# First attention blocks with one wide exponential after the transposition, row sums from a column of ones, batched scalings, signs partly on GpSimd, and another order

## The chip, the cores and the metric

The program runs on one core of one Trainium2 chip. The metric is the device time of one execution in microseconds (us); the time of a kernel is the median of its runs, and smaller is better. TensorE is called PE here, VectorE DVE, ScalarE ACT, GpSimd Pool, and SyncE, which only issues transfers, SP.

## The reference

A windowed attention over 4 batches, 8 heads, 576 positions and 64 channels feeds two feed-forward layers, each with a 512 x 2048 and a 2048 x 512 matrix. All inputs are float32.

```python
scores = (q @ k.T) / sqrt(64)
# heads 0-3: the last 32 positions; heads 4-7: every 4th of the last 128
scores = where(mask, scores, -1e9)
attn = exp(scores - max(scores)); attn = attn / (sum(attn) + 1e-9)
x = concat_heads(attn @ v)                 # 2304 tokens x 512
h = x @ w_in1;  y = (relu(h) ** 2) @ w_out1
h = y @ w_in2;  out = (h * sigmoid(h)) @ w_out2
```

## The kernel before

**Arithmetic.** Inputs of the feed-forward matrices arrive as pairs of 32-bit words and are turned into float32 on the chip; then each float32 matrix is split into a high and a low part of type fp32r, and each product is three matmuls (high x high, high x low, low x high). `weights` (L375 on) does this for one piece of 128 x 512: `top` (L394/L396, ACT or Pool) scales the upper word, L409 (DVE) shifts it left by 3, L411 (DVE) puts the sign bit in, `low` (L402, ACT) scales the lower word, L414 adds the two (DVE or Pool), L360/L364 copy the high part (ACT or Pool), L367 subtracts to get the low part (DVE or Pool). There are 64 pieces, 32 for each layer.

**Attention.** It is cut into 32 blocks: 8 halves of a batch (`h`, 288 positions each) by 4 pairs of heads (`pair`). A block has 3 units of 96 queries (plain heads) or 4 units of 72 queries (dilated heads), and two heads (`par`). Before the change, `attention` does for each block: scores (L563, PE) of all units of both heads; for each head and unit a masked minimum of the negated scores (L585, DVE), then an exponential with that minimum as bias, which also gives the row sum (L590, ACT); for each head one addition (L594), one reciprocal (L596) and for each unit a scaling (L604 ACT, L606 DVE or Pool); the transposition of each unit (L613, PE); a copy of the transposed probabilities out of PSUM (L360 ACT or L362 DVE); and one group of products with the values for both heads (L635, PE), whose result is split into high and low parts of `x`.

**Feed-forward.** Layer 0 has six tiles of tokens, three of 256 (`mlp`: lines L711 to L713 and L759 to L761) and three of 512, layer 1 has four of 512 and one of 256 (`mlp2`: lines L859 and L913 to L915). The first three tiles run while the weights are still being converted, so they run interleaved, each a fixed lag behind the one before. Tile 0 needs half 0 of the attention, tile 1 half 1, tile 2 half 2. From tile 3 on, converted weights are read back from memory.

**Order.** Every operation is an `Op` with a cost for each engine that can do it. `Planner.order` plays the program through with these costs when the kernel is built, takes at each step what can start first (the `key`, multiplied by `KEY_W`, decides near ties), chooses the engine, and so fixes the order on every engine. `lock` marks DVE operations that the planner doesn't let overlap with Pool. A load with a `gate` isn't issued before a given step of the feed-forward part. Up to `FILL_END`, when PE would sit idle in the plan, `fill` puts in matmuls on a tile of zeros (`warm`, L961) whose result nobody reads. `HINTS` moves single operations to an engine or shifts their key. Buffers come from pools: `raw` has 4, `ax` banks of PSUM 3.

Of the kernel before, what the change touches and what calls it, by code (L numbers as in the profile page):

```python
# [10 lines left out]
F32 = mybir.dt.float32  # L11
# [8 lines left out]
BLK_BUFS, BLK_COLS = 2, 1216  # L20
# [16 lines left out]
HOLDS = {"w0": "u4", "wa": "u4", "ws": "u4", "wb": "u4", "wc": "u2", "h": "u4", "xr": "u4", "xo": "u2", "cw": "u2", "raw": "u4", "ap": "u4", "x": "u4", "x2": "u4", "g4": "u4", "st": "u4",  # L37
# [24 lines left out]
def block_cols(half, pair):  # L62

    units = attn_units(half, pair)
    nk = max(u[2] + u[3] for u in units)
    return HALF, nk, len(units) * P
# [29 lines left out]
class Op:  # L96
    def __init__(self, engines, fn, deps, key, allocs, uses):
        self.engines, self.fn, self.key = engines, fn, key
        self.deps = [d for d in deps if d is not None]
        self.allocs, self.uses = allocs, uses  # L100
        tags = [g for b in allocs for g in b.tags]
        self.wants = [(g, tags.count(g)) for g in dict.fromkeys(tags)]
        self.start = self.end = self.eng = self.gate = None
        self.pace, self.full, self.lock = False, True, False
        for b in allocs:
            b.alloc_op = self


class Planner:
# [25 lines left out]
    def order(self):  # L135
# [90 lines left out]
        out, left_n = [], len(self.ops)  # L226
# [3 lines left out]
        while left_n:  # L230
            left_n -= 1
            best = None
            for e, r in ready.items():
                pick = None
                for o, t in r.items():
                    t = at(o, e, t)
                    if t is not None and all(t + o.engines[e] <= at(o, f, ready[f][o]) + d + 1e-9
                                             for f, d in o.engines.items() if f != e):
                        c = (t + KEY_W * o.key, o.seq)
# [11 lines left out]
            o.end = run(t, o.engines[e], o.full) if e == "PE" and t < FILL_END else t + o.engines[e]  # L251
# [58 lines left out]
class Kern:  # L310
    def __init__(self, ctx, tc, qkv, w1, w2, out):
# [10 lines left out]
        for h in range(NH):  # L322
            for pair in range(NPAIR):
                self.off[h, pair] = o
                cq, ck, cv = block_cols(h % 2, pair)
# [44 lines left out]
    def weights(self, m, c, key, dkey, js=(0, 1)):  # L370
# [3 lines left out]
        for j in js:  # L374
# [16 lines left out]
            def top(e, cv=cv, pair=pair):  # L391
# [3 lines left out]
                else:  # L395
                    nc.gpsimd.tensor_scalar(out=cv.tile, in0=x, scalar1=2.0 ** -112, scalar2=1.0,  # L396
                                            op0=ALU.mult, op1=ALU.mult)

            def low(e, pair=pair):
# [3 lines left out]
                else:  # L403
                    nc.gpsimd.tensor_scalar(out=x.bitcast(I32), in0=x, scalar1=2.0 ** -29, scalar2=1.0,
                                            op0=ALU.mult, op1=ALU.mult)

            a = self.op({"ACT": c_act(n) + 0.05, "Pool": c_pool1(n)}, top, [load], k, [cv], [raw], "v" + at)
            z = self.op({"ACT": c_act(n) + 0.05, "Pool": c_pool1(n)}, low, [load], k, [], [raw], "z" + at)
            b = self.op({"DVE": c_dve2(n)}, lambda e, vi=vi: nc.vector.tensor_scalar(  # L409
                out=vi(), in0=vi(), scalar1=3, scalar2=None, op0=ALU.logical_shift_left), [a], k, [], [cv], lock=True)  # L410
            s = self.op({"DVE": c_dve(n)}, lambda e, vi=vi, pair=pair: nc.vector.scalar_tensor_tensor(  # L411
                out=vi(), in0=pair(I32)[:, :, 1], scalar=-2147483648, in1=vi(),
                op0=ALU.bitwise_and, op1=ALU.bitwise_or), [b], k, [], [cv, raw], lock=True)
# [8 lines left out]
            h = self.op({"ACT": c_act(n), "Pool": c_pool1(n)}, lambda e, hv=hv, cs=cs: self.copy(e, hv(), cs()),  # L422
                        [w], k, [both], [cv], "h" + at)
# [95 lines left out]
    def load_blk(self, h, pair, key):  # L519
        nc = self.nc  # L520
        cq, ck, cv = block_cols(h % 2, pair)
# [9 lines left out]
        else:  # L531
# [8 lines left out]
            self.blk[h, pair] = parts[0], [(b, cq, o), (b, cq + ck, o)], parts[1]  # L540

    def attention(self, h, pair, key, step):
# [10 lines left out]
        pp = self.spot("ap", 1024)  # L553
        sp = self.buf("ast", 4, 24, rows=PL_Q)
# [16 lines left out]
        else:  # L571
            s = self.op({"PE": 0.1 + 0.26 * nu if h == 0 else 0.92}, scores, deps, key, sbanks + [pp, sp], use)
            s.full = h == 0
            ss = [s, s]
        for par in range(2):
# [6 lines left out]
            for i, (q0, n, k0, nk, m0) in enumerate(units):  # L582
# [6 lines left out]
                            [s], k + 0.1, [], [sbank, p, st])  # L589
                es.append(self.op({"ACT": c_act(nk) + 0.185}, lambda e, i=i, n=n, c=c, p=p, st=st: nc.scalar.activation(  # L590
                    out=p.tile[:n, c], in_=p.tile[:n, c], func=AF.Exp, scale=-1.0, bias=st.tile[:n, i:i + 1],
                    accum_out=st.tile[:n, 4 + i:5 + i]), [t], k + 0.2, [], [p, st]))
            d = lambda st=st: st.tile[:nq, 8:8 + nu]
# [4 lines left out]
            for i, (q0, n, k0, nk, m0) in enumerate(units):  # L598
                c = slice(i * P, i * P + nk)

                def norm(e, i=i, n=n, c=c, p=p, st=st):
                    x, f = p.tile[:n, c], st.tile[:n, 8 + i:9 + i]
                    if e == "ACT":
                        nc.scalar.activation(out=x, in_=x, func=AF.Copy, scale=f)  # L604
                    else:
                        self.eng[e].tensor_scalar(out=x, in0=x, scalar1=f, scalar2=1.0, op0=ALU.mult, op1=ALU.mult)  # L606

                ns.append(self.op({"Pool": 0.243 + 0.84e-3 * nk, "DVE": c_dve2(nk), "ACT": c_act(nk)}, norm,
                                  [r], k + 0.4, [], [p, st], f"n{at}.{i}", True))
# [27 lines left out]

        k = key + 2 * step
        o = self.op({"PE": 0.75}, pv, pts[0][1] + pts[1][1] + [dv], k,
                    [xb], [bv, pts[0][0], pts[1][0]])  # L640
        self.attended = [o]
# [4 lines left out]
        for t, lo, hi in parts:  # L646
# [33 lines left out]
            a.tagname = f'x{h}.{pair}'  # L680

# [12 lines left out]
    def mlp(self, m, tiles):  # L694
# [3 lines left out]
        for c, ti in sorted(((c, ti) for c in range(NF) for ti in range(len(tiles))), key=lambda x: tiles[x[1]][1](x[0])):  # L698
# [32 lines left out]
            def prod(e, r=r, bank=bank, n=n):  # L731
                if e == "Pool":
                    nc.gpsimd.tensor_tensor(out=r.tile, in0=r.tile, in1=r.tile, op=ALU.mult)
# [7 lines left out]
            b = self.op({"DVE": c_dve(n), "Pool": c_pool2(n)}, prod, [a], k + 0.2, [],  # L741
# [89 lines left out]
    def mlp2(self, m, t, k0, fetched):  # L831
# [7 lines left out]
        for f in range(NF // 2):  # L839
# [47 lines left out]
            for i, (hp, deps, own) in enumerate(parts):  # L887
# [6 lines left out]
                if m == 0:  # L894
                    b = self.op({"DVE": c_dve(n)}, lambda e, r=r, src=src: nc.vector.scalar_tensor_tensor(  # L895
                        out=r.tile, in0=src(), scalar=0.0, in1=src(), op0=ALU.max, op1=ALU.mult),
                        deps, k, [r], [own], f"p{at}.{i}", n == 512)
                else:
# [3 lines left out]
                        out=r.tile, in0=src(), in1=r.tile, op=ALU.mult), [a], k, [], [r, own], f"p{at}.{i}", n == 512)  # L902
# [25 lines left out]
    def constants(self, e):  # L928
        nc = self.nc
        self.ident = self.sb.tile([PL_Q, PL_Q], F32, name="ident")  # L930
        self.mask = self.sb.tile([PL_Q, P], F32, name="mask")
        make_identity(nc, self.ident)
        nc.gpsimd.memset(self.mask, 0.0)
# [6 lines left out]
    def run(self):  # L940
# [54 lines left out]
        for t in range(FIRST, len(TILES[0])):  # L995
# [5 lines left out]
            else:  # L1001
                for c in range(NF):
                    self.weights(1, c, k + 2 * c + 3, k + 2 * c - 1, (1,))
# [11 lines left out]
W_KEY = 4.0  # L1015
A_LEAD = 38.0
B_LEAD = 6.0
A1 = -5.0
A2 = 6.0
A2S = 4.0  # L1020
A3S = 3.0
B_LAG = 14.0
# [3 lines left out]
X_LEAD = 14  # L1026
X1_LEAD = 14
S1_FROM = 27.44
S1_STEP = 3.5
W1_BACK = 40  # L1030
# [4 lines left out]
A0S = 3.0  # L1035
W_STEP = 3.5
W0D = -46.0
B1 = -41.5
A1S = 5.5
W2_FROM = 60.0  # L1040
W2_STEP = 6.0
ENG = {"v": ("Pool", "ACT"), "z": ("ACT",), "w": ("DVE", "Pool"), 
       "h": ("ACT", "Pool"), "S": ("DVE", "Pool"), "l": ("Pool", "DVE"), "n": ("Pool", "ACT", "DVE"), "t": ("ACT", "DVE"), "x": ("DVE", "ACT"), "gh": ("ACT",), "gl": ("DVE", "Pool"), "p": ("DVE",)}
MOST = {"w0": 16, "wa": 3, "ws": 6, "wb": 2, "wc": 3, "h": 1, "xr": 2, "xo": 1, "cw": 2, "raw": 4, "ap": 3, "x": 8, "x2": 14, "g4": 4, "st": 2, "g2": 4, "cv": 3, "r": 2, "yo": 2, "stg": 3}
# [5 lines left out]
    "A5.0": ("", -8.0),  # L1050
    "B3.3": ("", -1.0),
    "R0.4.0": ("", -4.0),
    "gl0.0.10": ("Pool", 0),
    "gl0.5.3.1": ("Pool", 0),
    "h0.14.1": ("", -1.0),
    "n7.3.0.1": ("", 2.0),
    "n7.3.1.3": ("ACT", 0),
    "p0.3.3.1": ("", -1.0),
    "t0.0.1.0": ("", -8.0),
    "v0.15.1": ("ACT", 0),  # L1060
    "xh0.4.b21": ("", 16.0),
    "xh1.3.t2": ("", -2.0),
# [71 lines left out]
```

## Time and profile before

| | us |
|---|---|
| median of 3 runs | 906.86 |
| lowest, highest | 906.71, 909.58 |
| profiled execution, whole | 909.49 |
| profiled execution, span | 907.7 |
| PE busy in the span | 888.2 |
| DVE, ACT, Pool busy | 662.7, 455.0, 78.9 |

The span is what the profiler recorded from the first to the last instruction; 1.8 us of the profiled execution's time lie around it. A busy PE also counts the matmuls on zeros.

### The profile page before, as it was taken

How to read it: one execution, taken by the hardware profiler on the slowest of the kernel's cores; microseconds unless marked ns; L12 is line 12 of the kernel's file. 1: busy time of each engine (PE TensorE's matmuls, PEld its weight loads, DVE VectorE, ACT ScalarE, POOL GpSimd, SP SyncE). 2: the span in 40 equal slices, each digit the busy share in tenths (PEclk: the TensorE clock that was granted, in tenths of full speed). 3: DMA queues.
4: the chain of work that ended last, by engine and by line, in shares of the span. 5: the costliest groups of instructions: out<-in, count | busy, mean ns of one | idle time of the engine just before them, and what ended most of it. 6: DMA issues, size and time to landing. Idle time of an engine off the chain costs nothing.

```text
span 907.7 us, 18193 instructions
## 1 busy us (share of the span) xinstructions
PE 888.2 (98%) x6589; PEld 806.3 (89%) x6589; DVE 662.7 (73%) x1749; ACT 455.0 (50%) x1260; POOL 78.9 (9%) x97
## 2 busy tenths in 40 slices
PE   8999999999999999999999999999999999999998
PEld 6888988999878988899999899999999899999998
DVE  6999999997787798787989986475448445545422
ACT  6979887867675366343454553233225222323222
POOL 1442122110110100010010100000000000000000
PEclk9999999999999999999999999999999999999999
DMA  8487677667989989878889974557565656645060
GB/s 303 157 251 260 206 255 251 238 216 259 335 283 337 344 288 321 310 253 312 306 323 351 368 264 163 200 183 249 170 221 193 201 174 242 244 136 175 26 210 25
DMA packets 75738, 217.92 MB, mean 240 GB/s; under 512 B 8576, under 2 KB 20096, under 8 KB 75648
## 3 DMA queue, kind: packets, MB, share of 16 engines
q1 hardware_dynamic: 75648, 216.76, 68.6%
q8 instruction: 52, 0.85, 0.4%
q14 instruction: 38, 0.31, 0.1%
HBM read 170.59 MB, written 46.14 MB: 239 GB/s over the span
## 4 chain that ended last, share of the span: by engine, by line
PE 74%; DVE 14%; ACT 6%; DMA 4%; issue 2%; SPq 0%; POOL 0%; ACTq 0%; DVEq 0%; POOLq 0%
PE s L859 32%; PE y L913 12%; PE y L914 12%; PE y L915 12%; ACT ap L590 2%; DMA raw<-w 2%; DVE st L367 1%; ACT ap L604 1%; PE ax L961 1%; DVE st L466 1%; DVE g L367 1%; DVE ap L585 1%; DVE ap L606 1%; DVE r L735 1%; DMA x<-xo 1%
## 5 line engine op out<-in xcount | busy, mean ns | idle before, releaser
L875 DVE TENSOR_TENSOR h<-s,h 128x512 f32<-128x512 f32 x224 | 139.5, 623 | 135.2 <-PE s L859 121.7
L913 PE MATMUL y<-g,w 128*128 128x512 f32 (+1 forms) x512 | 194.5, 380 | 0.0
L914 PE MATMUL y<-g,w 128*128 128x512 f32 (+1 forms) x512 | 193.2, 377 | 0.0
L915 PE MATMUL y<-g,w 128*128 128x512 f32 (+1 forms) x512 | 192.8, 377 | 0.0
L859 PE MATMUL s<-x,ws 128*128 128x256 f32 x1344 | 172.4, 283 | 0.7 <-DVE ap L362 0.6
L859 PEld LDWEIGHTS s<-x,ws 128*128 128x128 f32 x1344 | 166.0, 192 | 1.4 <-DVE ap L362 0.7
L360 ACT CAST g<-r 128x512 fp32r<-128x512 f32 (+1 forms) x176 | 94.2, 542 | 58.5 <-DVE r L895 29.0
L915 PEld LDWEIGHTS y<-g,w 128*128 128x128 f32 x512 | 96.4, 188 | 18.4
L913 PEld LDWEIGHTS y<-g,w 128*128 128x128 f32 x512 | 96.5, 188 | 16.1
L914 PEld LDWEIGHTS y<-g,w 128*128 128x128 f32 x512 | 96.5, 189 | 15.3
L367 DVE TENSOR_TENSOR g<-r,g 128x512 fp32r<-128x512 f32 (+1 forms) x170 | 99.5, 605 | 13.8 <-ACT g L360 10.2
L859 PE MATMUL s<-x,wa 128*128 128x256 f32 x768 | 105.0, 285 | 2.0 <-issue 2.0
L859 PEld LDWEIGHTS s<-x,wa 128*128 128x128 f32 x768 | 100.8, 192 | 6.7 <-issue 2.4
L899 ACT ACTIVATE r<-h 128x512 f32<-128x512 f32 x64 | 37.1, 625 | 133.4 <-DVE h L875 133.4
L590 ACT ACTIVATE ap<-ap,ast 96x128 f32<-96x128 f32 (+3 forms) x224 | 82.6, 372 | 17.7 <-DVE ast L585 17.6
L711 PE MATMUL s<-x,w 128*128 128x256 f32 x192 | 56.7, 295 | 3.0 <-DVE ast L585 1.5
L873 ACT COPY h<-s 128x256 f32<-128x256 f32 x56 | 20.7, 370 | 74.5 <-PE s L859 73.1
L901 DVE TENSOR_TENSOR r<-h,r 128x512 f32<-128x512 f32 x64 | 41.5, 689 | 22.6 <-ACT r L899 22.6
L713 PE MATMUL s<-x,w 128*128 128x256 f32 x192 | 54.4, 284 | 0.7 <-DVE w L367 0.7
L712 PE MATMUL s<-x,w 128*128 128x256 f32 x192 | 54.1, 282 | 0.0
L859 PE MATMUL s<-x,wc 128*128 128x256 f32 x336 | 49.3, 282 | 0.0
L402 ACT ACTIVATE raw<-raw 128x512 int32<-128x512 uint32 x64 | 42.6, 678 | 4.6 <-DMA raw<-w 4.6
(110 smaller groups left out, 1452.9 us busy)
## 6 DMA issues: line engine op xcount, KB each, us to landing
raw<-w SPq DMA_DIRECT2D x64, 512.0 KB, 7.2
ws<-w2x SPq DMA_DIRECT2D x64, 512.0 KB, 4.7
ws<-w1x SPq DMA_DIRECT2D x48, 512.0 KB, 6.6
wa<-w2s SPq DMA_DIRECT2D x40, 512.0 KB, 4.2
wa<-w1s SPq DMA_DIRECT2D x24, 512.0 KB, 6.2
w1s<-w SPq DMA_DIRECT2D x16, 512.0 KB, 4.2
w1x<-st SPq DMA_DIRECT2D x16, 512.0 KB, 3.7
w2s<-st SPq DMA_DIRECT2D x16, 512.0 KB, 4.8
```

The source lines that it names most:

```text
L360: self.nc.scalar.copy(out=out, in_=in_)
L367: self.eng[eng].tensor_tensor(out=out, in0=a, in1=b, op=ALU.subtract)
L402: nc.scalar.activation(out=x.bitcast(I32), in_=x, func=AF.Copy, scale=2.0 ** -29)
L590: es.append(self.op({"ACT": c_act(nk) + 0.185}, lambda e, i=i, n=n, c=c, p=p, st=st: nc.scalar.activation(out=p.tile[:n, c], in_=p.tile[:n ...
L711: nc.tensor.matmul(o, wh.tile[:, s], xh, start=(kk == 0), stop=False)
L712: nc.tensor.matmul(o, wh.tile[:, s], xl, start=False, stop=False)
L713: nc.tensor.matmul(o, wl.tile[:, s], xh, start=False, stop=(kk == KC - 1))
L859: nc.tensor.matmul(bank.tile[:, o:o + 256], wp, xp, start=i == 0, stop=last, skip_group_check=True)
L875: add = lambda o, a, b: nc.vector.tensor_tensor(out=o, in0=a, in1=b, op=ALU.add)
L913: nc.tensor.matmul(o, wh.tile[:, s], gh.tile, start=c == 0, stop=False)
L914: nc.tensor.matmul(o, wh.tile[:, s], gl.tile, start=False, stop=False)
L915: nc.tensor.matmul(o, wl.tile[:, s], gh.tile, start=False, stop=(c == NF - 1))
```

## The change

- In the first 8 blocks (halves 0 and 1, `EARLY`), the exponentials move behind the transposition (`late_exp`). PE transposes the shifted scores and adds, in the same PSUM bank, a matmul that subtracts each row's minimum (a column of `ast`, broadcast, times `minus`, the negated identity). One exponential then covers all units of a head that have the same number of keys, reads PSUM and writes SBUF; it has no bias pointer and no row sum. The copy out of PSUM goes away.
- The values of these blocks carry a column of ones for each unit and head (`ones`, a memset), so that the product with the values gives 64 columns and the row sum; it is done for each head apart and comes out with the queries on the partitions. The addition and the reciprocal are as before; one multiplication for each head scales the result of all units into `xn`, and PE transposes it back (`turn`).
- In the other 24 blocks, scalings of units with the same number of keys are one operation; on DVE one multiplication by a broadcast column.
- In `weights`, the operation L409 can go to Pool: it then clears the upper word except for its sign, and the shift is done by DVE together with the sign. `top`, `low` and the high copy can go to DVE too. The square of layer 0's first tiles can go to ACT, no longer to Pool.
- The planner takes 0.17 us off a PE operation that follows one of the same `kind` (scores, and the last PE step of a block) and favours it by 0.31 us in its choice; fillers also wait for an `ax` bank. Leads, lags and the 16 hints are replaced; there are now about a hundred hints.

```diff
-BLK_BUFS, BLK_COLS = 2, 1216
+BLK_BUFS, BLK_COLS = 2, 1224
+EARLY = 8
...
-                t = max(free["PE"], vacant(tag, "PE"))
+                t = max(free["PE"], vacant(tag, "PE"), vacant("ax", "PE"))
...
-                        c = (t + KEY_W * o.key, o.seq)
+                        c = (t + KEY_W * o.key - (STAY if o.kind and o.kind == kind else 0), o.seq)
...
-            o.end = run(t, o.engines[e], o.full) if e == "PE" and t < FILL_END else t + o.engines[e]
+            d = o.engines[e] - (SWITCH if o.kind and o.kind == kind else 0)
+            o.end = run(t, d, o.full) if e == "PE" and t < FILL_END else t + d
...
+            def shift(e, vi=vi, pair=pair):
+                x = pair(U32)[:, :, 1].bitcast(F32)
+                if e == "DVE":
+                    nc.vector.tensor_scalar(out=vi(), in0=vi(), scalar1=3, scalar2=None, op0=ALU.logical_shift_left)
+                else:
+                    nc.gpsimd.tensor_scalar(out=x, in0=x, scalar1=0.0, scalar2=1.0, op0=ALU.mult, op1=ALU.mult)
+            b = self.op({"DVE": c_dve2(n), "Pool": c_pool1(n)}, shift, [a], k, [], [cv, raw], "b" + at, True)
+            def sign(e, vi=vi, pair=pair, b=b):
+                x = pair(I32)[:, :, 1]
+                if b.eng == "DVE":
+                    nc.vector.scalar_tensor_tensor(out=vi(), in0=x, scalar=-2147483648, in1=vi(),
+                                                   op0=ALU.bitwise_and, op1=ALU.bitwise_or)
+                else:
+                    nc.vector.scalar_tensor_tensor(out=vi(), in0=vi(), scalar=3, in1=x,
+                                                   op0=ALU.logical_shift_left, op1=ALU.bitwise_or)
...
+            if early(h, pair):
+                pts.append(self.late_exp(units, p, st, tbank, es, k, at, par, bv, ov, dv, xn))
+                continue
...
+                    if e == "DVE" and j > i + 1:
+                        nc.vector.tensor_tensor(out=x, in0=x, in1=f.unsqueeze(2).to_broadcast([n, j - i, nk]), op=ALU.mult)
+                        return
...
+        def turn(e):
+            for i, (q0, n, k0, nk, m0) in enumerate(units):
+                nc.tensor.transpose(xb.tile[:, q0:q0 + n], xn.tile[:n, i * P:i * P + P], self.ident[:n, :n])
...
+        if early(h, pair):
+            o = self.op({"PE": 0.25}, turn, pts + [self.ident_op], k, [xb], [xn])
+        else:
+            o = self.op({"PE": 0.75}, pv, pts[0][1] + pts[1][1] + [dv], k,
+                        [xb], [bv, pts[0][0], pts[1][0]])
+        o.kind = 1
...
+    def late_exp(self, units, p, st, tbank, deps, k, at, par, bv, ov, dv, xn):
+        nu, nq = len(units), units[0][1]
+        full = max(((i, u[3]) for i, u in enumerate(units)), key=lambda x: (x[1], -x[0]))
+        def transp(e):
+            for i, (q0, n, k0, nk, m0) in sorted(enumerate(units), key=lambda u: -u[1][3]):
+                o = tbank.tile[:nk, q0:q0 + n]
+                nc.tensor.matmul(o, p.tile[:n, i * P:i * P + nk], self.ident[:n, :n], is_transpose=True,
+                                 start=(i, nk) == full, stop=False, skip_group_check=True)
+                nc.tensor.matmul(o, st.tile[:n, i:i + 1].to_broadcast([n, nk]), self.minus[:n, :n],
+                                 start=False, stop=True, skip_group_check=True)
...
+            es.append(self.op({"ACT": c_actp(c.stop - c.start)}, lambda e, c=c, nk=units[i][3]: nc.scalar.activation(
+                out=p.tile[:nk, c], in_=tbank.tile[:nk, c], func=AF.Exp, scale=-1.0), [t], k + 0.3, [], [tbank, p]))
...
+                nc.tensor.matmul(vb.tile[:n, 65 * i:65 * i + 65], p.tile[:nk, q0:q0 + n], bv.tile[:nk, v0:v0 + 65],
+                                 start=True, stop=True)
...
+            if e == "DVE":
+                nc.vector.tensor_tensor(out=x, in0=v()[:, :, :64], in1=d().unsqueeze(2).to_broadcast([nq, nu, 64]), op=ALU.mult)
+                return
+            for u in range(nu):
+                nc.scalar.activation(out=x[:, u], in_=v()[:, u, :64], func=AF.Copy, scale=d()[:, u:u + 1])
...
-X_LEAD = 14
+STAY = 0.31
+SWITCH = 0.17
+X_LEAD = 39.0
...
-B1 = -41.5
+B1 = -31.16
...
-W2_FROM = 60.0
+W2_FROM = 49.2
```

## Rows read from the trace of the kernel before

**Rows 1.** The page: busy time, share of the span and instructions of each engine.
```profile
PE 888.2 (98%) x6589; PEld 806.3 (89%) x6589; DVE 662.7 (73%) x1749; ACT 455.0 (50%) x1260; POOL 78.9 (9%) x97
```

**Rows 2.** Windows: stretch, length; busy of PE, PEld, DVE, ACT, POOL; PEclk, DMA share, GB/s.
```profile
0.00:80.00 80.00, 74.65 (x757) 63.41 (x758) 69.63 (x333) 65.52 (x260) 25.77 (x34) 1.00 0.71 236
80.00:300.00 220.00, 211.86 (x1909) 195.54 (x1908) 196.34 (x683) 160.53 (x531) 32.08 (x40) 1.00 0.77 267
520.00:860.00 340.00, 340.00 (x2138) 308.89 (x2138) 193.13 (x310) 109.84 (x203) 4.06 (x5) 1.00 0.56 192
...
20.00:30.00 10.00, 9.46 (x106) 7.38 (x106) 9.41 (x55) 9.27 (x40) 3.35 (x4) 1.00 0.05 20
```

**Rows 3.** Groups of PE instructions by line, 0 to 80 us.
```profile
L961 PE MATMUL ax<-warm 128*128 128x256 bf16 x237 | 30.9, 281 | 1.1 <-DVE warm L952 1.1
```

**Rows 4.** Timeline of PE: start, length, line and operation.
```profile
4.02 2.61 PE L563 MATMUL y<-w 128*96 128x96 f32 x24
8.78 1.23 PE L563 MATMUL y<-w 128*72 128x72 f32 x16 [2.14 <-DMA w<-qkv]
...
30.06 0.72 PE L635 MATMUL ax<-ap,blk 128*64 128x96 f32 x12
30.70 0.39 PE L711 MATMUL s<-x,w 128*128 128x256 f32 x1
30.92 0.28 PE L712 MATMUL s<-x,w 128*128 128x256 f32 x1
...
35.99 0.90 PE L563 MATMUL ax<-blk 64*96 64x128 f32 x12
36.82 0.39 PE L759 MATMUL y<-g,w 128*128 128x256 f32 x1
...
40.98 0.66 PE L613 MATMUL ax<-ident,ap 96*128 96x96 f32 x6
41.48 0.82 PE L961 MATMUL ax<-warm 128*128 128x256 bf16 x6
```

**Rows 5.** Timeline of ACT: two exponentials of plain heads, one of dilated heads.
```profile
6.02 0.39 ACT L590 ACTIVATE ap<-ap,ast 96x128 f32<-96x128 f32 x1
...
6.41 0.39 ACT L590 ACTIVATE ap<-ap,ast 96x128 f32<-96x128 f32 x1
...
21.37 0.35 ACT L590 ACTIVATE ap<-ap,ast 72x72 f32<-72x72 f32 x1
```

**Rows 6.** Groups by line and shape, ACT, 0 to 100 us: copies out of PSUM.
```profile
L360 ACT COPY ap<-ax 72x288 f32<-72x288 f32 x8 | 3.1, 393 | 0.0
L360 ACT COPY ap<-ax 128x192 f32<-128x192 f32 x7 | 2.3, 327 | 0.0
```

**Rows 7.** Groups by line and shape, DVE: 0 to 300 us, 0 to 80, 0 to 100.
```profile
L409 DVE TENSOR_SCALAR cv<-cv 128x512 int32<-128x512 int32 x38 | 15.8, 433 | 0.5 <-ACT cv L394 0.3
...
L606 DVE TENSOR_SCALAR ap<-ap,ast 96x128 f32<-96x128 f32 x17 | 5.0, 324 | 0.0
...
L367 DVE TENSOR_TENSOR x<-ax,x 128x192 fp32r<-128x192 f32 x4 | 1.7, 432 | 0.4 <-ACT x L360 0.4
```

**Rows 8.** Timelines of DVE (two additions of one shape), of Pool; Pool's group, 0 to 100.
```profile
10.73 0.64 DVE L594 TENSOR_SCALAR ast<-ast 96x3 f32<-96x3 f32 x1
...
13.23 0.15 DVE L594 TENSOR_SCALAR ast<-ast 96x3 f32<-96x3 f32 x1
...
10.70 0.65 POOL L396 TENSOR_SCALAR cv<-raw 128x512 f32<-128x512 f32 x1 [8.60 <-DMA raw<-w]
...
L396 POOL TENSOR_SCALAR cv<-raw 128x512 f32<-128x512 f32 x14 | 13.0, 929 | 28.4 <-DMA raw<-w 20.0 <-PE y L761 4.4 <-DVE cv L409 4.0
```

**Rows 9.** Timeline of PE around 512 us, and windows there.
```profile
512.33 1.57 PE L859 MATMUL s<-x,wa 128*128 128x256 f32 x6 [1.99 <-issue]
...
512.00:514.00 2.00, 1.67 (x7) 1.70 (x8) 2.00 (x5) 1.96 (x4) 0.00 (x0) 0.60 0.97 370
514.00:516.00 2.00, 2.00 (x6) 1.52 (x6) 2.00 (x4) 0.38 (x1) 0.00 (x0) 0.55 0.70 209
```

More of the change, by code (lines that the diff above doesn't have):

```diff
@@ L403, in low @@
                 else:
[L404 removed]
+                    self.eng[e].tensor_scalar(out=x.bitcast(I32), in0=x, scalar1=2.0 ** -29, scalar2=1.0,
                                             op0=ALU.mult, op1=ALU.mult)
[L407 to L408 removed]
@@ L409, in weights @@
[L409 to L413, printed above, removed]
+            a = self.op({"ACT": c_act(n) + 0.05, "Pool": c_pool1(n), "DVE": c_dve2(n)}, top, [load], k, [cv], [raw], "v" + at, True)
@@ new lines, in weights @@
+            z = self.op({"ACT": c_act(n) + 0.05, "Pool": c_pool1(n), "DVE": c_dve2(n)}, low, [load], k, [], [raw], "z" + at, True)
+            def shift(e, vi=vi, pair=pair):
[4 more added lines that the diff above has]
+                    nc.gpsimd.tensor_scalar(out=x, in0=x, scalar1=0.0, scalar2=1.0, op0=ALU.mult, op1=ALU.mult)
@@ L414, in weights @@
+            s = self.op({"DVE": c_dve(n)}, sign, [a, b], k, [], [cv, raw], lock=True)
             w = self.op({"DVE": c_dve(n), "Pool": c_pool2(n)}, lambda e, vi=vi, pair=pair: self.eng[e].tensor_tensor(
@@ new lines @@
+    "gh0.0.9": ("ACT", 4.0),
+    "gh0.1.12": ("", 1.0),
+    "gh0.2.7": ("ACT", 0),
+    "gh0.4.3.0": ("", 2.0),
+    "gh0.5.0.0": ("Pool", 0),
+    "gh0.5.1.1": ("", -1.0),
+    "gh0.5.2.1": ("Pool", -4.0),
+    "gh0.5.3.1": ("", -8.0),
+    "gl0.0.12": ("", -21.0),
+    "gl0.0.13": ("DVE", 0),
+    "gl0.0.6": ("", 4.0),
+    "gl0.1.15": ("", -16.0),
+    "gl0.1.5": ("Pool", 0),
+    "gl0.1.6": ("", 8.0),
+    "gl0.2.1": ("DVE", 0),
+    "gl0.2.14": ("DVE", -1.0),
+    "gl0.2.2": ("DVE", 0),
@@ new lines @@
+    "t7.0.0.0": ("", -12.0),
+    "t7.0.1.0": ("DVE", 0),
+    "t7.2.1.0": ("DVE", 4.0),
+    "v0.0.0": ("Pool", 0),
+    "v0.1.1": ("DVE", 0),
+    "v0.6.0": ("", -2.0),
+    "x0.0.1": ("ACT", 0),
+    "x0.3.0": ("", 1.0),
+    "x1.0.2": ("", 1.0),
+    "x1.3.2": ("DVE", 0),
+    "x2.1.2": ("ACT", 0),
+    "x3.2.o": ("ACT", 0),
+    "x3.3.o": ("", 4.0),
+    "xh0.3.b11": ("", -16.0),
+    "xh0.3.t1": ("", -3.0),
+    "xh0.4.b11": ("ACT", 16.0),
+    "xh0.5.b21": ("", -4.0),
+    "xh0.5.b22": ("Pool", 0),
@@ L1066 @@
+    "xh1.0.t3": ("ACT", 0),
+    "xh1.0.t4": ("ACT", 0),
+    "xh1.1.b22": ("", -1.0),
+    "xh1.3.b22": ("Pool", 0),
+    "xl0.3.b22": ("DVE", 14.0),
+    "xl0.3.t1": ("DVE", 0),
+    "xl1.3.t1": ("DVE", 0),
+    "xs0.3.1": ("DVE", 0),
+    "xs0.4.0": ("Pool", 0),
+    "xs1.0.3": ("", 4.0),
+    "z0.1.0": ("", 2.0),
+    "z0.10.1": ("DVE", 0),
+    "z0.12.1": ("ACT", 0),
+    "z0.14.0": ("ACT", 0),
+    "z0.6.0": ("", -5.0),
+    "z0.6.1": ("", 16.0),
+    "z0.8.1": ("", 16.0),
 }
```

242 lines of the change are left out of this document (176 added, 66 removed).

## The prediction, written before the change was run

> **What bounds the kernel now.** I read the busy times first. PE is busy for 888.2 of 907.7 us and every other engine for much less [rows 1], so the reader's first thought should be that PE's own work sets the time, and the second what of that "busy" is work. The windows come next, because an average over stages with different limits says nothing of the first 100 us. From 520 to 860 us PE is busy for 340.0 of 340 us [rows 2]: there only PE's own instructions could gain. What PE loses lies elsewhere: 80.00 - 74.65 = 5.35 us before 80 us, 220.00 - 211.86 = 8.1 us from 80 to 300 [rows 2], 2.0 us near 511 [rows 9], and the other 4.1 of 907.7 - 888.2 = 19.5 us elsewhere, which the change doesn't touch. The groups by line then show what the windows hide: 237 matmuls on zeros, 30.9 us, all before 80 us [rows 3]. So before 80 us PE spends 30.9 + 5.35 = 36.2 us on nothing, and this is the largest sum that anything could win.
>
> Who holds PE up there is seen in the same windows: DVE is busy for 69.6 and ACT for 65.5 of the first 80 us, and DVE for 196.3 of the 220 us after that [rows 2]. PE's timeline shows that the first matmul of the feed-forward part starts only at 30.70 us [rows 4]: until then ACT takes the exponentials one by one, one every 0.39 us for 96x128, and 0.35 us long for 72x72 [rows 5]. The transfers are not the limit: from 20 to 30 us their share is 0.05 [rows 2], since the buffers of raw weights stay full until ACT and DVE have converted them. So the ramp up to 80 us is bounded by the work of ACT and DVE together, and all after it by PE.
>
> **The change, part by part.** Exponentials: the first 8 blocks have 24 units of plain heads, counted by head (8 passes of 3), and 32 of dilated heads (8 passes of 4). 24 x 0.39 + 32 x 0.35 = 20.6 us of ACT [rows 5]. The wide form has not been seen; its nearest rows are ACT's copies out of PSUM of the same shapes, 0.393 for 72x288 and 0.327 for 128x192 [rows 6]. Four passes need 96 and 192 columns, twelve need 288: with 0.327 for each of the short ones, 8 x 0.327 + 12 x 0.393 = 7.3 us. An exponential is bounded below by these copies and above by what it costs today, 0.39 for 128 columns, so 1.17 for three times as much; I take the copies, since neither bias nor row sum is left. Removed: 13.3 us (20.6 less 16 x 1.17 is 2, so 2 to 13). The copies themselves fall away, another 7.3 us of ACT or DVE.
>
> Scalings: 56 operations of up to 0.32 us [rows 7], say 0.26 since most are shorter and neighbours overlap, are 14.6 us. In their place stand 16 multiplications out of PSUM of 192 or 256 columns; the nearest row is 0.432 for 192 columns [rows 7], so about 0.48 each and 7.7 us. Removed: 6.9 us (2 to 9). Additions and reciprocals stay. Eight memsets of ones are new; they can go to Pool, which is busy for 25.8 of 80 us, and cost nothing unless they hold up DVE; without that cover they are 8 x 0.15 = 1.2 us by the smallest DVE row [rows 8].
>
> Signs: each operation L409 that goes to Pool takes 0.43 us from DVE; 38 of the 64 run before 300 us [rows 7], by their even spacing some 14 in the ramp. I take half of these, 3 us (from a loss, see the second rival, to 6).
>
> Sum for ACT and DVE: 13.3 + 7.3 + 6.9 + 3 = 30.5 us, 15 for each engine if the planner balances them, which the freer choice of engines for `top`, `low` and the high copy allows. The ramp would end at 65 instead of 80 us.
>
> PE gets more to do. A matmul that subtracts the minimum is a float32 matmul, two records: 30.70 - 30.06 = 0.64 us for 12 records in the product with the values, 0.83 for 12 in the scores [rows 4], so 0.107 to 0.138 each, and 56 of them are 6.0 to 7.7; I take 7. `turn` is 28 transpositions at (41.48 - 40.98) / 6 = 0.083, 2.3 us. Each block now visits PE six times instead of four. The first matmul after such a visit takes 0.39 us, the next 0.28 [rows 4]; with as much lost at the entry, a visit costs 2 x 0.11, say 0.2: 16 x 0.2 = 3.2. Products with the values keep their number. Added: 12.5 us (9 to 14).
>
> What covers it is the filler. If the ramp shrinks by 15, then 36.2 - 15 = 21.2 us of filler and idling are left, 12.5 of them are filled with the new work, and 8.7 remain. The start alone takes 4.02 us until the first scores and 2.14 of waiting for the second pair's input [rows 4], so 6.2 cannot go at all: the two limits, ACT with DVE and PE, would meet almost exactly. Such a fit is never reached, since PE waits for a chain (minimum, transposition, exponential, product, scaling, transposition back) and the ramp is short; I take two thirds, 10.5 us. Bounds: 0, if PE's new work takes the place of useful work rather than filler, and 36.2 - 12.5 - 6.2 = 17.5.
>
> Order: putting scores next to the last step of another block saves 0.2 us each time. 24 blocks run after the ramp; I take ten such meetings, 2 us (0 to 24 x 0.2 = 4.8). The batched scalings of these blocks and further signs on Pool relieve DVE from 80 to 300 us, where PE lacks 8.1 us; part of that is chain latency, so I take 0 of it (0 to 8). Earlier loads for the second layer (`X_LEAD`, `W2_FROM`) queue on SP ahead of other loads; what they read was written long before, and PE has no gap from 520 to 860 us that they could close or open, so 0.
>
> The sum is 10.5 + 2 = 12.5 us less. Against the profiled execution: 909.5 - 12.5 = 897.0. That execution is 2.6 us above the median, and it holds a stall that may not belong to the others: PE idle for 1.99 us before 512.33 for no reason that the profile shows, then 4 us at a granted clock of 0.60 and 0.55 [rows 9], near the lower level of 1.2 GHz of 2.4. So I take the difference from the median: 906.9 - 12.5 = 894.4, say 894.5 us.
>
> **The rivals.** First, the cover is not there: PE's 12.5 us land between feed-forward matmuls that were ready. For it: all of it sits in a ramp that becomes PE's own limit when it shrinks. Against it: 36.2 us of nothing are there now. Then 15 - 12.5 = 2.5 is gained, with the order some 4: 903.
>
> Second, on the other side, Pool blocks DVE. The addition at 10.73 us took 0.64 us, the same one at 13.23 us 0.15; the slow one began 0.03 us after a Pool operation of 0.65 us and ended with it [rows 8]. So DVE stood still for 0.49 us while Pool ran. A sign on Pool saves DVE 0.43 and costs it what Pool blocks, up to 0.93, the mean of Pool's operation of that size [rows 8]. If each of the 38 before 300 us blocked for its whole length, DVE would lose 38 x (0.93 - 0.43) = 19 us there, and with DVE as the limit the result is 894.5 + 19 = 913.5. Signs on Pool are a loss once 0.43 / 0.93, about half, of their time blocks DVE; from (0.43 + 12.5 / 38) / 0.93 = 0.82 on the whole change is slower. Against it: the planner keeps marked operations apart, and Pool's 25.8 us before 80 [rows 2] left DVE's L409 at a mean of 0.43. The Trainium skill says it harder (SBUF — State Buffer, on the shared port pair): the pair that DVE and GpSimd share is an exclusive lock, held for a whole instruction, and the second to start is blocked fully. The addition at 10.73 us agrees with that rule. If every sign met such an operation, the sum by the rule would be the 913.5 above; by the row of L409, whose mean shows few such meetings, it stays 894.5.
>
> Third, the clock falls: real work is short and scattered where fillers stood. After the 1.99 us stall 2 x 0.40 + 2 x 0.45 = 1.7 us were lost to the lower level [rows 9]; seven or eight such falls would eat the gain (907). The granted clock is 1.00 in the first 300 us [rows 2], and fillers remain allowed. The added transpositions are only 2.3 us. The Trainium skill (TensorE: Matmul & The Clock Gate, PE-mode transpose) holds that transpositions don't count as activity for the clock gate in the way other matmuls do; no row here shows it.
>
> Fourth, more is won: the ramp reaches its bound of 17.5 and the order its 4.8: 884.6.
>
> **How the numbers follow.** Forecast (890 to 900): 0.50. Cover missing (900 to 906): 0.22. More won (under 890): 0.13. Pool (over 907): 0.11. Clock (about 907): 0.04. The range of 8 in 10 reaches from 884, the fourth case's bound, to 907, which leaves out the Pool case, half of the clock's, and a little below 884; the forecast's own range is 890 to 900. About 0.3%, or 2.7 us, can be told from no change. Faster than 904.1: forecast, more won, and most of the missing cover, 0.82; within: 0.07; slower than 909.6: 0.11.
>
> **What would show it.** Right: ACT's wide exponentials take 0.3 to 0.4 us, the feed-forward part starts near 22 us instead of 30.70, fillers fall from 237 to under 100, and PE is filled from about 65 us on; from 300 us on all rows are the old ones, shifted by some 12 us. Wrong: a first feed-forward matmul still near 30 us (the chain, not the throughput, set the start), fillers gone but float32 matmuls longer than 0.14 us (first rival), DVE's small operations at 0.5 us and more (second), a granted clock under 1.00 before 100 us (third). My sum fails most easily at the two thirds of the ramp.

## The result, and the profile after

The changed kernel takes 896.04 us (median of 4 runs, 892.34 to 898.78) against 906.79 us for the kernel before, run beside it; the ratio is 0.9873, with a 95% interval of 0.9831 to 0.9914. So it is faster by 10.8 us by the medians, and by 7.8 to 15.3 us by the interval, where 12.5 had been forecast. Its runs spread over 6.4 us. The profiled execution took 898.78 us, with a span of 897.0; it is the longest of the four, as the profiled one before was 2.6 us above its median.

The page's busy times [rows 1] show PE still on top and ACT relieved:

```profile
PE 881.0 (98%) x6546; PEld 807.6 (90%) x6546; DVE 648.7 (72%) x1660; ACT 422.9 (47%) x1123; POOL 92.1 (10%) x103
```

The windows of the changed kernel (columns as in [rows 2]), the ramp first, then the stretches after it:

```profile
0.00:80.00 80.00, 73.95 (x729) 68.39 (x731) 63.20 (x298) 52.04 (x157) 27.14 (x38) 0.94 0.74 255
80.00:300.00 220.00, 216.07 (x1954) 201.54 (x1955) 194.42 (x641) 159.47 (x527) 40.85 (x38) 1.00 0.81 279
500.00:520.00 20.00, 19.27 (x124) 17.23 (x122) 17.32 (x33) 9.54 (x17) 1.27 (x2) 1.00 0.68 260
520.00:860.00 340.00, 338.77 (x2132) 307.39 (x2133) 185.16 (x299) 105.57 (x199) 2.54 (x3) 1.00 0.56 192
```

Before 80 us ACT has 13.5 us less to do and DVE 6.4 [rows 2]. PE idles 80.00 - 73.95 = 6.05 us there instead of 5.35, so a reader of busy shares would see no gain in the ramp. The groups of PE by line, 0 to 80 us, show what the share hides: the fillers fell from 237 [rows 3] to 54, and the matmuls that subtract the minima stand in their place. (Their 16.2 us overlap the transpositions between them; counted from the start of each instruction to the start of the next, they take 11.5 us.)

```profile
L1079 PE MATMUL ax<-warm 128*128 128x256 bf16 x54 | 8.3, 314 | 1.1 <-DVE warm L1070 1.1
L758 PE MATMUL ax<-minus,ast 96*128 96x96 f32 (+3 forms) x112 | 16.2, 265 | 0.0
```

From 80 to 300 us PE idles for 3.9 us instead of 8.1. The stall near 511 us [rows 9] is not there: 0.7 us of idling from 500 to 520, with a clock of 1.00.

Counted on PE's timeline from start to start (idle is what no instruction covers), these are PE's us in the first 300:

| | before | after | no_minus | start | no_hints | nh_no_late |
|---|---|---|---|---|---|---|
| feed-forward | 193.3 | 202.8 | 205.6 | 208.8 | 202.4 | 193.2 |
| attention | 64.2 | 79.6 | 70.9 | 75.2 | 75.2 | 65.3 |
| of it, subtracting minima | 0 | 11.5 | 0 | 10.5 | 10.8 | 0 |
| fillers | 29.0 | 7.6 | 8.5 | 7.6 | 10.6 | 24.7 |
| idle | 13.5 | 10.0 | 15.1 | 8.4 | 11.8 | 16.9 |
| first feed-forward matmul at | 30.70 | 30.02 | 28.43 | 26.33 | 24.86 | 29.69 |

(The other columns are experiments, below.) The change removes 24.9 us of fillers and idling and adds 15.4 us of attention; PE has done 9.5 us more of the feed-forward part at 300 us, which is nearly all of the gain. Split at 80 us, the same count shows where it was won:

| | before, 0 to 80 | after, 0 to 80 | before, 80 to 300 | after, 80 to 300 |
|---|---|---|---|---|
| feed-forward | 21.1 | 23.2 | 172.2 | 179.6 |
| attention | 24.5 | 43.1 | 39.7 | 36.5 |
| fillers | 29.0 | 7.6 | 0 | 0 |
| idle | 5.4 | 6.1 | 8.1 | 3.9 |

In the ramp 20.7 us of fillers and idling went, but attention took 18.6 of them, and only 2.1 us became feed-forward work. The other 7.4 us were won from 80 to 300 us: 4.2 less idling and 3.2 less attention.

The prices, one group each: ACT's wide exponentials by shape, DVE's scalings into `xn`, both 0 to 80 us, and the signs by Pool and what is left of the shifts on DVE, both 0 to 300 us.

```profile
L769 ACT ACTIVATE ap<-ax 72x288 f32<-72x288 f32 x4 | 1.6, 406 | 4.3 <-PE ax L758 4.2
L769 ACT ACTIVATE ap<-ax 128x192 f32<-128x192 f32 x4 | 1.3, 325 | 0.0
...
L790 DVE TENSOR_TENSOR xn<-ax,ast 72x256 f32<-72x256 f32 x8 | 3.3, 418 | 0.1
L790 DVE TENSOR_TENSOR xn<-ax,ast 96x192 f32<-96x192 f32 x6 | 2.1, 350 | 0.1
...
L425 POOL TENSOR_SCALAR raw<-raw 128x512 f32<-128x512 f32 x24 | 23.2, 969 | 43.4 <-ACT cv L403 40.6 <-issue 1.2 <-DVE cv L405 1.0
...
L423 DVE TENSOR_SCALAR cv<-cv 128x512 int32<-128x512 int32 x16 | 7.1, 444 | 0.0
```

A wide exponential of 288 columns costs 0.406 us, hardly more than the one of 128 columns with bias and row sum [rows 5]. And 24 of the 40 signs before 300 us went by Pool, 10 of 16 in the ramp, where the prediction had reckoned with 7.

The first matmul of the feed-forward part starts at 30.02 us, not near 22. PE's timeline and the windows (the column after POOL's is the granted clock) show where the time went:

```profile
7.61 0.39 PE L758 MATMUL ax<-minus,ast 96*128 96x96 f32 x2
7.83 0.25 PE L756 MATMUL ax<-ident,ap 96*128 96x96 f32 x1
...
10.89 0.77 PE L778 MATMUL ax<-w,ap 96*96 96x65 f32 x6 [1.47 <-ACT ap L769]
11.49 0.26 PE L756 MATMUL ax<-ident,ap 96*128 96x96 f32 x1
...
16.67 3.22 PE L602 MATMUL y<-w 128*72 128x72 f32 x32
...
30.02 0.37 PE L827 MATMUL s<-x,w 128*128 128x256 f32 x1
...
10.00:12.00 2.00, 1.11 (x11) 1.11 (x12) 0.49 (x1) 1.37 (x5) 1.30 (x2) 0.99 1.03 411
12.00:14.00 2.00, 2.00 (x14) 2.00 (x13) 1.53 (x7) 1.03 (x4) 0.46 (x1) 0.50 1.05 418
14.00:16.00 2.00, 2.00 (x13) 2.00 (x13) 1.49 (x5) 1.01 (x3) 0.49 (x2) 0.50 1.03 421
16.00:18.00 2.00, 2.00 (x18) 2.00 (x18) 1.22 (x6) 0.46 (x2) 0.00 (x0) 0.50 1.04 416
18.00:20.00 2.00, 2.00 (x27) 2.00 (x25) 1.15 (x14) 0.00 (x0) 0.00 (x0) 0.80 1.01 406
...
59.22 1.06 PE L778 MATMUL ax<-blk,ap 104*72 104x65 f32 x10 [1.14 <-ACT ap L769]
...
60.00:64.00 4.00, 4.00 (x32) 3.87 (x32) 3.18 (x9) 1.79 (x5) 0.40 (x1) 0.60 0.48 165
```

PE waits 1.47 us for an exponential, then the granted clock is 0.50 for more than 6 us, though PE is busy all the time. It falls once more after a wait of 1.14 us, again for an exponential, to a mean of 0.60 from 60 to 64 us. For the first fall the timelines of ACT and DVE show what stood in the way at the start: an operation stands ahead of the exponentials on ACT and one ahead of the masked minima on DVE, and each waits for a transfer.

```profile
10.04 0.67 ACT L411 ACTIVATE raw<-raw 128x512 int32<-128x512 uint32 x1 [8.02 <-DMA raw<-w]
10.60 0.81 ACT L769 ACTIVATE ap<-ax 96x96 f32<-96x96 f32 x4
...
6.79 0.06 DVE L575 MEMSET w<- 128x6 f32 x1 [5.79 <-DMA w<-qkv]
6.88 0.25 DVE L626 CUSTOM_DVE_ANT_0 ap<-y,mask 96x96 f32<-96x96 f32 x1
```

### The profile page after: what moved, and what is told of

It is laid out like the page before. It is cut to its first block, busy times and chain, and to the rows that moved or that the text cites. A ratio compares the mean times of both kernels' runs of the same rounds, so it can differ in the third digit from the quotient of the medians.

```text
span 897.0 us, 17882 instructions
## 1 busy us (share of the span) xinstructions
PE 881.0 (98%) x6546; PEld 807.6 (90%) x6546; DVE 648.7 (72%) x1660; ACT 422.9 (47%) x1123; POOL 92.1 (10%) x103
## 5 line engine op out<-in xcount | busy, mean ns | idle before, releaser
L376 DVE TENSOR_TENSOR g<-r,g 128x512 fp32r<-128x512 f32 (+1 forms) x171 | 101.1, 608 | 19.0 <-ACT g L369 15.3
L634 ACT ACTIVATE ap<-ap,ast 96x128 f32<-96x128 f32 (+3 forms) x168 | 61.9, 370 | 9.8 <-DVE ast L626 9.6
L989 ACT COPY h<-s 128x256 f32<-128x256 f32 x56 | 20.7, 370 | 76.8 <-PE s L975 76.7
L411 ACT ACTIVATE raw<-raw 128x512 int32<-128x512 uint32 x51 | 34.6, 682 | 26.0 <-DMA raw<-w 25.9
```

The lines of the kernel that those rows point to most:

```text
L376: self.eng[eng].tensor_tensor(out=out, in0=a, in1=b, op=ALU.subtract)
```

## The experiments

Each has its ratio to the kernel before, run beside it on the same chip; medians of different chips are best compared by these ratios. The change's own interval is wide, 3.8 us each way, so that a difference from it of less than about 4 us is not clear of the noise.

| label | median us | ratio, 95% interval |
|---|---|---|
| the change | 896.0 | 0.9873 (0.9831 to 0.9914) |
| no_late | 907.9 | 0.9978 (0.9960 to 0.9997) |
| old_tuning | 918.3 | 1.0099 (1.0074 to 1.0124) |
| old_tuning_no_late | 913.7 | 1.0052 (1.0031 to 1.0072) |
| no_minus | 897.3 | 0.9861 (0.9836 to 0.9887) |
| start | 893.3 | 0.9830 (0.9810 to 0.9851) |
| signs_dve | 911.4 | 1.0039 (1.0012 to 1.0066) |
| no_kind | 900.8 | 0.9920 (0.9904 to 0.9937) |
| no_hints | 899.6 | 0.9910 (0.9890 to 0.9930) |
| nh_no_late | 909.1 | 1.0001 (0.9980 to 1.0021) |
| nh_signs_dve | 907.2 | 0.9977 (0.9960 to 0.9993) |
| nh_norms_apart | 905.3 | 0.9950 (0.9926 to 0.9974) |
| start_no_minus | 896.4 | 0.9848 (0.9823 to 0.9874) |

**no_late.** The late exponentials undone.

```diff
-EARLY = 8
+EARLY = 0
```

> The changed kernel with EARLY = 0: exponentials, scalings and transposition of all 32 blocks as before the change; signs on Pool, batched scalings, new leads and new hints stay. Theory A (the wide exponentials relieve ACT and DVE while the weights are converted, and this is most of the gain): ACT has about 13 us more and the copies 7 us more to do before 80 us, fillers come back to over 150, and the time is 902 to 908 us. Rival B (the gain comes from the retuned order, the signs on Pool and the batched scalings, and the late exponentials give PE about as much as they take): 893 to 899 us, with some 15 us less attention work on PE.

0.9978: theory A by the time. Without the late exponentials only 0.2% of the time is gained. The fillers come back, 197 of them. ACT's load rises by 7.4 us only, where 13 and up to 7 for the copies had been expected. The window of its ramp, at a clock of 0.91:

```profile
0.00:80.00 80.00, 70.94 (x689) 59.83 (x691) 65.61 (x308) 59.41 (x230) 20.26 (x32) 0.91 0.65 221
```

**old_tuning** and **old_tuning_no_late.** The new code with the old leads, lags, choices of engine and hints; the second has the late exponentials undone too.

```diff
-W_KEY = 6.78
+W_KEY = 4.0
...
-STAY = 0.31
-SWITCH = 0.17
+STAY = 0.0
+SWITCH = 0.0
...
-ENG = {"b": ("DVE", "Pool"), "v": ("Pool", "ACT", "DVE"), ...
+ENG = {"b": ("DVE",), "v": ("Pool", "ACT"), ...
```

> The changed kernel's code with the late exponentials and the batched scalings, but with all leads, lags, choices of engine and hints of the kernel before, signs on DVE, no preference for a kind. Theory A (late exponentials alone carry the gain): 895 to 901 us. Rival B (they only pay with the new order): 902 us or more, up to slower than the kernel before, because PE's 15 us of added work meet gaps that the old order does not fill.

> As old_tuning, but with EARLY = 0 too: of the change only the batched scalings of all blocks are left. Both theories: DVE saves at most 7 us spread over 300 us, PE's work is that of the kernel before, so 904 to 909 us. If it were under 902, the batched scalings would carry a part that neither theory gives them.

Rival B holds for this pair: 1.0099 with the late exponentials, 1.0052 without. The second had been expected near the kernel before: without the late exponentials, the rest of the new code under an order not made for it costs 0.0052 x 907 = 4.7 us. And late exponentials without signs on Pool and without the new order are no gain: they lose another 0.0047 x 907 = 4.3 us.

**no_minus.** The subtracting matmul left out, the order kept.

```diff
-                                 start=(i, nk) == full, stop=False, skip_group_check=True)
-                nc.tensor.matmul(o, st.tile[:n, i:i + 1].to_broadcast([n, nk]), self.minus[:n, :n],
-                                 start=False, stop=True, skip_group_check=True)
+                                 start=(i, nk) == full, stop=True, skip_group_check=True)
```

> The changed kernel in its own order, without the matmuls that subtract each row's minimum in the first 8 blocks (the exponentials there are of scores that are not shifted). They took 11.5 us of PE's time before 80 us in the profile, counted from start to start, against 7 that the prediction put down. Theory C (the ramp is now PE's own limit): 5 to 9 us less than the changed kernel, 887 to 891 us, and the first feed-forward matmul well before 30 us. Rival D (the chain of DVE, ACT and PE in the first blocks sets the start, PE's share is covered): within 2 us of the changed kernel, and PE waits where the matmuls were, at a lower granted clock.

0.9861 against 0.9873: rival D. 11.5 us of PE's work vanish and the time stays. (The two intervals alone would still allow theory C's smallest gain, 5 us; start_no_minus, below, does not.) The window and PE's largest wait (us in total, times, longest) show what took their place: PE is busy for 5.1 us less, at a lower clock (0.91 against 0.94), and waits for the exponentials.

```profile
0.00:80.00 80.00, 68.89 (x637) 61.75 (x637) 63.84 (x301) 53.27 (x160) 28.67 (x39) 0.91 0.75 262
...
PE ax L776 <- ACT ap L767: 7.9, 6, 1.9
```

**start.** Two operations moved behind the work that they held up: the conversion `z0.0.0` behind the fourth wide exponential, the memset `o0.0` behind the last masked minimum of the second block. ACT's table load came to stand before the first exponential with them.

```diff
-        for o in self.pl.order():
+        ops = self.pl.order()
...
+        for name, last in (("z0.0.0", self.marks["e0.0.1"]), ("o0.0", self.marks["t0.1.1"])):
...
+                o = ops.pop(i)
...
+                ops.insert(j, o)
+        for o in ops:
             o.fn(o.eng)
```

> The changed kernel with two operations moved in the order of their engines, nothing else: the first conversion of a lower word on ACT goes behind the first four wide exponentials (it waits for a transfer until 10.04 us and holds them back to 10.60), and the first memset of ones on DVE goes behind the masked minima (it waits for a transfer until 6.79 us). Theory E (in-order blocking at the start costs PE 1.5 us at 6.8 us and 1.5 us at 10.9 us, and the second gap lets the clock fall to 0.50 for some 6 us, which costs 3 us more): the granted clock stays at 1.00 to 20 us, the first feed-forward matmul comes at 25 to 27 us instead of 30.02, and the time falls by 3 to 6 us. Rival F (the conversion of weights by DVE sets the ramp, whatever PE does before 30 us): the clock stays up, but the time changes by less than 2 us.

0.9830 against 0.9873: 893.3 us, the lowest median here. The clock stays at 1.00 up to 20 us, as theory E said, and the first feed-forward matmul comes at 26.33 us. The median is lower by 2.7 us, by the ratios 3.9, near theory E's lower end; but the two intervals overlap, so that the gain in time is likely but not shown. PE's timeline, its windows, and ACT's timeline:

```profile
9.10 0.65 PE L780 MATMUL ax<-w,ap 96*96 96x65 f32 x6
9.59 0.25 PE L757 MATMUL ax<-ident,ap 96*128 96x96 f32 x1
...
26.33 0.37 PE L829 MATMUL s<-x,w 128*128 128x256 f32 x1
...
12.00:14.00 2.00, 0.98 (x10) 0.91 (x11) 1.93 (x8) 1.43 (x4) 0.62 (x1) 1.00 1.04 414
16.00:18.00 2.00, 2.00 (x33) 2.00 (x32) 1.90 (x25) 0.41 (x1) 0.00 (x0) 1.00 1.04 416
...
8.44 0.46 ACT L770 ACTIVATE ap<-ax 96x96 f32<-96x96 f32 x2 [0.56 <-PE ax L759]
```

The product with the values starts at 9.10 instead of 10.89 us. A later gap of 1.04 us, in the window from 12 to 14, did not take the clock down. The changed kernel's second fall, from 60 to 64 us, is not there either: the clock is 1.00 over the whole 80 us.

**signs_dve.** All shifts on DVE.

```diff
-ENG = {"b": ("DVE", "Pool"), ...
+ENG = {"b": ("DVE",), ...
```

> The changed kernel with the shift L423 on DVE for all 64 pieces, as in the kernel before; the planner makes its order anew. In the profile of the changed kernel 10 of 16 signs before 80 us go by Pool. Theory G (signs on Pool relieve DVE, which is busy for 18 to 20 of every 20 us up to 120 us): DVE has 10 x 0.41 = 4 us more before 80 us, and the time is 2 to 5 us above the changed kernel's. Rival H (Pool's operations block DVE for as long as they save): within 2 us, or faster, and the small operations of DVE get shorter on the mean.

1.0039: 15 us lost, far beyond theory G's 2 to 5. Most of the loss lies after the ramp; from 80 to 300 us PE idles for 13.0 us instead of 3.9:

```profile
80.00:300.00 220.00, 206.99 (x1832) 192.02 (x1832) 190.64 (x638) 156.96 (x523) 19.03 (x18) 0.98 0.77 266
```

**no_kind.** No preference for PE operations of one kind.

```diff
-STAY = 0.31
-SWITCH = 0.17
+STAY = 0.0
+SWITCH = 0.0
```

> The changed kernel with STAY = SWITCH = 0: the planner neither favours nor discounts a PE operation of attention that follows another one. In the profiles PE visits attention 81 times before 310 us in the kernel before and 74 times in the changed one, though each of its first 8 blocks needs six steps instead of four. Theory I (each merged visit is worth 0.2 us): 20 to 25 visits more, 4 to 5 us above the changed kernel. Rival J (merging delays other work by as much): within 2 us.

0.9920, 4.3 us above the change by the ratios, just at the edge of the noise. The size is theory I's, its count is not: PE visits attention 77 times before 310 us, counted by the starts of its instructions, against 73 in the changed kernel by the same count, and not 20 to 25 times more. So merged visits don't explain the loss; hints that no longer fit may.

**no_hints.** The list of hints emptied.

> The changed kernel with an empty list of hints; code, leads and lags as changed. Theory K (the structure carries the gain, the hints only trim it): within 4 us of the changed kernel, 895 to 900 us. Rival L (the hints carry a large part, as old_tuning's 918 us suggests, where the same structure met a list that was not made for it): 903 us or more.

0.9910: theory K. The hints, 128 by the list, are worth 3.4 us by the ratios, which is within the noise. Since this kernel has no list made for it, it is a fairer base for taking parts away, though leads and lags are still those of the full change:

**nh_no_late, nh_signs_dve, nh_norms_apart.** no_hints with one part undone each: the edits of no_late and of signs_dve, and one scaling for each unit:

```diff
-                while j < nu and units[j][3] == units[i][3]:
-                    j += 1
+                j = i + 1
```

> no_hints (899.6 us, ratio 0.991) with EARLY = 0, so that neither of the two has a list made for the other. no_late was 908 us, but its hints had been made for a kernel with late exponentials. Theory A (late exponentials save ACT some 20 us and DVE 7 us at the start, and this is worth most of the gain): 905 to 912 us. Rival M (most of no_late's 12 us came from hints that no longer fitted): within 4 us of no_hints, 896 to 903 us.

> no_hints with all shifts on DVE. In no_hints 27 of 40 signs before 300 us go by Pool, in signs_dve none did, and that was 911 us. Theory G (27 x 0.41 = 11 us of DVE's time before 300 us, where DVE is busy for nine tenths and PE waits for it): 905 to 911 us. Rival M (signs_dve suffered from unfitting hints): 897 to 903 us.

> no_hints with one scaling for each unit in the 24 later blocks, as before the change. The batched form saves DVE at most some 0.15 us for each head, 7 us in all, most of it from 60 to 280 us. If DVE's time there counts as in theory G, 2 to 6 us above no_hints; if the scalings are spread over Pool and ACT where there is room, within 2 us of it.

The losses are 0.0091, 0.0067 and 0.0040 of 907 us: 8.3 us for the late exponentials, 6.1 for the signs on Pool, 3.6 for the batched scalings. Each is uncertain by 2 to 3 us. For the first two theory A and theory G hold by the time. For the third the loss lies in the range given for DVE's time counting, but the traces don't bear that reading out: the edit leaves the first 8 blocks as they are, and yet the first feed-forward matmul comes at 30.14 us instead of 24.86 and PE has done 4.3 us less of the feed-forward part at 80 us. The planner's new order at the start thus probably holds a part of the 3.6 us, and what the batched scalings are worth is not shown. The three sum to 18 us where no_hints has won 8.2 in all, so the parts are not independent: with any of the first two missing, nearly nothing is won.

**start_no_minus.** The edits of start and of no_minus together.

> start (893.3 us, ratio 0.983) without the matmuls that subtract the row minima in the first 8 blocks (the exponentials there are of scores that are not shifted). In no_minus these 11 us of PE turned into waiting for ACT, at a lower granted clock. Theory D (PE's added work is covered also when ACT is not held up at the start): within 2 us of start. Rival C (with the start mended PE's own work before 30 us is the limit): 3 to 6 us below start, 887 to 890 us.

0.9848 against start's 0.9830, 1.6 us above it, uncertain by 3: theory D again, and theory C's 3 to 6 us below are excluded. PE's added work is covered even there. The windows of start and of start_no_minus show that part of what the matmuls left went to a lower clock, 0.96 against 1.00, which over 80 us is some 3 us of full-clock PE time:

```profile
0.00:80.00 80.00, 76.28 (x806) 70.56 (x806) 69.07 (x314) 58.49 (x172) 30.23 (x40) 1.00 0.81 280
0.00:80.00 80.00, 68.97 (x658) 61.64 (x659) 66.42 (x305) 55.28 (x164) 29.82 (x39) 0.96 0.78 271
```

## Why the prediction was right, by its steps

The number was right; of the mechanism a part was, and two misses of the sum balanced each other.

**The bound.** It held that ACT and DVE set the ramp and PE all after it. That PE's added work doesn't set the ramp is shown: taking it off again changes nothing (no_minus, start_no_minus). That ACT's and DVE's work sets it is supported, not shown alone: giving them their old work back takes all of the gain (nh_no_late, 1.0001), but the order changes with it, and of the 9.2 us of feed-forward work that nh_no_late lacks against no_hints at 300 us only 3.6 are lacking at 80 us. The second half was too simple. From 80 to 300 us PE idles for 13.0 - 3.9 = 9.1 us more with all shifts on DVE (signs_dve), and for 10.9 - 7.1 = 3.8 us more in nh_signs_dve against no_hints.

**The prices.** Exponentials were right: 0.406 and 0.325 us where the copies gave 0.393 and 0.327 [rows 6]. Scalings came out at 0.35 and 0.42 instead of 0.48. The relief as a whole was put too high: ACT and DVE are busy for 13.5 + 6.4 = 19.9 us less in the ramp, where 30.5 had been summed up; they began the signs of 16 pieces there instead of 15. The subtracting matmul was mis-sized: 7.83 - 7.61 = 0.22 us for 96x128 where 0.138 was the upper bound, 11.5 us in all instead of 7, part of it at the lower clock (10.5 in start, whose clock is 1.00). One term was missed. The products with the values keep their number, but they changed their shape and cost more: (9.59 - 9.10) / 3 = 0.16 us each in start, where (30.70 - 30.06) / 6 = 0.11 had been read before [rows 4]; in the changed kernel the 56 of the early blocks take 9.8 us, against 5.6 at the mean of 0.10 before. So attention took 18.6 us more of PE before 80 us, where 12.5 had been put down.

**The cover.** Fillers and idling in the ramp fell by 20.7 us; the forecast needed 10.5 + 12.5 = 23. So the cover was there, as assumed, and no_minus and start_no_minus speak against the first rival. But nearly all of it was used up by attention.

**Where in time.** This step failed. The ramp was to give 10.5 us (called two thirds, though it is 0.7 of the 15 by which the ramp was to shrink), and it gave 2.1 us of feed-forward work. The stretch from 80 to 300 us, where the prediction had put 0 of a possible 8 and 2 for the order, gave 4.2 us of idling and 3.2 of attention. That 2.1 + 7.4 came near to 10.5 + 2 is luck, and with it that the time lies within the forecast's range. Three of the prediction's own signs of being wrong were there: a first feed-forward matmul near 30 us, float32 matmuls longer than 0.14 us, and a clock under 1.00 before 100 us.

The feed-forward part was to start near 22 us. It started at 30.02, and the order of the start is a part of the reason: in-order waits on ACT and DVE, and a clock of 0.50 after them; in start it is 26.33. An early start is not enough by itself: no_hints has 24.86 and 899.6 us. By an estimate from the windows, three at 0.50 and one at 0.80 cost 3 x 1.0 + 0.4 = 3.4 us of full-clock PE time, and the second fall 4 x 0.40 = 1.6 more. This is the third rival in small. PE was filled from about 65 us on, nearly as said: the last filler runs at 68.5 us, instead of 75.3.

**Signs.** They were forecast at 3 us of DVE's time in the ramp; by the time of the kernel nh_signs_dve shows 6.1 us and signs_dve 15, both with the misfit of a new order, the second with that of the hints too. The second rival did not come: 24 signs went by Pool, and the 16 shifts left on DVE have a mean of 0.444 us, against 0.433 [rows 7]. Over the first 300 us, 27 DVE operations that ran beside one of Pool's took over 0.2 us longer than the lower quartile of their kind (same operation, tiles and shape) before the change, 12.0 us in all; after it there are 22, with 9.5 us. So more work on Pool did not bring more blocking. It exists all the same, in single cases. The timelines of DVE and Pool of the changed kernel:

```profile
71.80 1.56 DVE L654 TENSOR_TENSOR ap<-ap,ast 72x288 f32<-72x288 f32 x1
76.44 0.44 DVE L654 TENSOR_TENSOR ap<-ap,ast 72x288 f32<-72x288 f32 x1
...
71.62 1.42 POOL L439 TENSOR_TENSOR cv<-cv,raw 128x512 int32<-128x512 int32 x1 [2.71 <-DVE ast L643]
```

The batched scaling that began 0.18 us after a Pool operation had begun took 1.56 us and ended 0.32 us after it; a later one, beside which Pool ran nothing, took 0.44. The Trainium skill (SBUF — State Buffer, Who interferes with whom) says that a DVE instruction with two inputs in SBUF contends with a GpSimd instruction that reads SBUF. The rows agree: both the scaling and Pool's addition read two tiles in SBUF.

**Order.** 2 us had been put down for ten merged visits. Attention from 80 to 300 us takes 3.2 us less with as many score matmuls in it, and most of that is in the transpositions, 8.2 us instead of 10.6. Visits before 310 us went from 81 to 73, but this counts visits that only fillers part; with fillers left out of the count they rose from 65 to 70, where the early blocks make 16 more steps. That the preference for a kind did this is not shown (no_kind has 77, and 73 without fillers).

**What stays open.** Every edit but those of no_minus, start and start_no_minus makes the planner write a new order, with leads tuned for the full change, so a part's price holds its misfit too; old_tuning_no_late, with little more than the batched scalings left of the change, lost 4.7 us. How much of 8.3, 6.1 and 3.6 us is misfit was not separated, and nh_norms_apart shows that it can be a large part.

## What to carry to other kernels

Where two engines hold up a third, count what the third does with its waiting: work moved onto it was free here as long as fillers and idling covered it, and taking it away again won nothing. Count it all the same, the products whose shape changes too: here it used up nearly the whole cover. And split a gain by stage: a sum can come out right with its parts wrong. In a hand-made order, look at the first microseconds of each engine for an operation that waits for a transfer ahead of work that is ready; two such moves brought the first feed-forward matmul 3.7 us forward and kept the clock up, and the time was lower by 2.7 to 3.9 us, which is not clear of the noise. Parts of a change that relieve the same bound should be tried together and under an order made for them: here the late exponentials under the old settings were a loss of 4.3 us, and under the new ones taking them out lost 8.3 us.

## What the runs showed of the hardware that had not been expected

After 1.47 us without work the granted clock was 0.50 from 12 to 18 us although PE was busy for 2.00 of every 2 us; what ran up to 16.67 us were transpositions and small float32 matmuls, and the clock came back, 0.80 from 18 to 20 us and 1.00 after it, when 32 records of score matmuls had begun at 16.67. After another wait of 1.14 us its mean was 0.60 from 60 to 64 us, with PE busy for 4.00 of 4 us, while a gap of 1.04 us in start left it at 1.00. What decides between the two is not shown.

A float32 matmul whose weights are one column, broadcast to 128, and whose moving side is 96 columns takes 0.22 us from start to start, more than the scores' 0.138 with 96 columns of weights and 128 moving ones [rows 4]. And the products with the values, with the probabilities as 96 columns of weights and 65 moving columns, take 0.16 us, where 64 columns of weights and 96 moving ones took 0.11 [rows 4].
